# First attention chunk, w_in block shape, planner constants and priorities changed in a fused attention, MoE and SoLU kernel

## The chip, the core and the metric

The kernel is one program on one core of a Trainium2 chip. Five engines work beside each other, each through its own list of instructions in the order in which they were emitted: TensorE (PE, with its weight loads as PEld), VectorE (DVE), ScalarE (ACT), GpSimd (POOL) and SyncE (SP), which here issues all DMAs. The metric is the device time of one execution in microseconds (us), the median of several runs.

## What is computed

Three layers follow one another. Everything is float32 at the program's edge; the products are made of a rounded high part and a low part of each operand.

```python
# q, k, v: (2, 8, 768, 64); proj: (64, 6)
q_bits = (einsum('bhsd,dk->bhsk', q, proj) > 0);  k_bits = same of k
q_bucket = sum(q_bits * 2**arange(6));  k_bucket = same
scores = where(q_bucket[..., :, None] == k_bucket[..., None, :], q @ k.T / 8, -1e9)
x = softmax(scores) @ v                      # to (1536, 512): 8 heads of 64
p = domain_probs / sum(domain_probs)         # 4 experts
y = sum_e p[:, e] * (relu(x @ w1[e]) @ w2[e])  # w1: 4 x 512 x 1024
h = y @ w_in                                 # 512 x 1024
z = h * softmax(h);  ln = (z - mean) / sqrt(var + 1e-6) * g_ln
out = ln @ w_out                             # 1024 x 512
```

## The kernel before

The 1536 tokens are four chunks of 384 (three tiles of 128 each); chunks 0 and 1 are batch 0, chunks 2 and 3 batch 1. Of each chunk the kernel does attention over eight heads, the four experts (`moe_a` is x @ w1, `moe_b` is h @ w2), then y @ w_in (`h2_piece`, `h2_mm`), the normalisation (`ln_tiles`) and the product with w_out (`ln_a`, `ln_b`). Attention of chunk 0 (`attn_first`) has nothing to run beside. Attention of chunk c + 1 (`attn_steps`, handed out by `fill`) is interleaved with the experts of chunk c. The last chunk ends in `last_layer`, which goes tile by tile.

**Chunk 0.** `proj_steps` takes one head at a time: POOL rounds k or q to its high part, DVE subtracts to get the low part (tile `hl`), PE transposes both, ACT copies them into a "stack" of high over low (`k_stk`, `q_stk`, which live in the buffers wsa, wsb, stk and kC), and PE multiplies the stack with `lhs_w` to get the hash bits, added up over a group of heads in one PSUM tile. When a group is whole, ACT and DVE turn it into rows of 0 and -C (k) or 1 and 0 (q) for 16 contraction rows per head (`k_br`, `q_br`: the tiles ee and vs, and qC). The group size is `GS`: heads 0 to GS - 1 are projected before the first head's scores, the others are steps of a generator (`rest`) that the first heads' rows call. `unit(h)` loads head h's second operands by DMA: kB from the stack's low part and the bits, qB likewise. Each row tile `rr` of a head then makes four matmuls of scores (two halves, stack and kB/qB), DVE takes the maximum (tile `sm`), ACT the exponential (tile `p`), POOL divides, PE transposes p, ACT and DVE write high and low part, and a head ends in 12 matmuls with v (tile `vs`). At `h == GS` the kernel stores all eight k stacks and their bits to the DRAM tile kD, for chunk 1.

**w_in.** It arrives as 64-bit numbers; `decode_a` writes it to the DRAM tile winD in four blocks. `Stream` loads a block into `wra`, ACT rounds it to the high part and DVE subtracts (`wsa`). `h2_mm(c, t, j, o)` uses block j for tile t: 12 matmuls of 256 columns.

**Order.** Nothing is issued while the functions run: `Recorder.add` notes every operation, and `emit` then plays a list schedule with assumed costs and hand-over times (`cost`, `HOPS`, and in `emit` the time for a DMA to land and an extra for results that TensorE waits for) and issues each engine's instructions in the order of that play. Which ready operation goes first is its place in the recording, less `ahead(...)`, plus `SHIFTS`: rows of (engine, first, end, places) that move all operations first to end. On the chip the order is then fixed; only semaphores delay an instruction.

All operations carry the line of `emit`'s last loop, L406, so the rows below tell them apart by tile: `xh,wsa` is `moe_a`, `wsb,hh` is `moe_b`, `wsa,xh` is `h2_mm`, `idr,hl` and `lhs_w` are the projections, `idn,p` the transposes of p, `idn,y` those of y, `idn,ln` those of the normalised tile.

Of the kernel before, what the change touches and what calls it, by code (L numbers as in the profile page):

```python
# [95 lines left out]
class Recorder:  # L96
# [198 lines left out]
    def emit(self):  # L295
# [46 lines left out]
        while len(order) < n:  # L342
# [9 lines left out]
            for e in ready:  # L352
# [26 lines left out]
                if e == "S":  # L379
                    free[e] = now + (1.2 if o["turn"] else 0.46)  # L380
                    wire = max(wire, now + 1.15) + (0.75 if o["turn"] else o["cost"])
                    done = wire + 0.85
# [9 lines left out]
                for j in users[i]:  # L392
# [3 lines left out]
                    if e != "T" and "T" in ops[j]["forms"]:  # L396
                        hop += 0.4
# [12 lines left out]
def lsh_attention_moe_solu(  # L410
# [34 lines left out]
    GS = 4  # L445
# [77 lines left out]
    def f(ap):  # L523
        return ap.bitcast(F32)
# [255 lines left out]
    def attn_first():  # L780

        c = 0
# [17 lines left out]
        load_k(2, GS)  # L800
# [73 lines left out]
        for h in range(H):  # L874
            nxt = unit(h + 1) if h + 1 < H else None
            if h == GS:
                rec.gate = marks[-1]
                for g in range(H):
                    SP.dma_start(out=kD[b][0:2 * D, g], in_=f(k_stk[g]))
                    SP.dma_start(out=kD[b][2 * D:LQ, g], in_=k_br[0 if g < GS else 1][g:128:H])  # L880
                rec.gate = None
# [80 lines left out]
    winD = dram.tile([FF2 // 256, 128, KD, 256], F32, name="winD")  # L962
# [45 lines left out]
    def decode_a():  # L1008
# [3 lines left out]
        for j in range(FF2 // n):  # L1012
            for kk in range(KD):
                dst = winD[j * n // 256:(j + 1) * n // 256, :, kk].rearrange("j p n -> p j n")
# [7 lines left out]
    class Stream:  # L1022
# [10 lines left out]

        def load(self, i):
            while self.nl <= min(i, len(self.items) - 1):
                t = wr_r[self.kind].next()
# [4 lines left out]
        def split(self, i):  # L1041
            while self.ns <= min(i, len(self.items) - 1):
                self.load(self.ns)
                w = self.place.get(self.ns) or ws_r[self.kind].next()
                t = self.raw.pop(self.ns)
# [139 lines left out]
    def h2_mm(c, t, j, o):  # L1185
        yh, yl = xT[c]
        wh, wl = W1.get(i1["in", c, j])
        ts = slice(t * 128, t * 128 + 128)
        m = 0
# [293 lines left out]
```

## Time and profile before

| | |
|---|---|
| median of 3 runs | 947.25 us (946.66 to 950.53) |
| profiled execution | 946.51 us, of it a span of 944.7 us from first to last instruction |
| PE busy | 900.8 us (95%), 4864 matmuls |
| DVE, ACT, POOL busy | 673.1, 612.0, 144.1 us |
| mean granted TensorE clock | 0.991 of full speed |

A row of a timeline tells when a run of equal instructions started, how long it lasted, and in brackets how long the engine sat idle before it and what ended that. Consecutive matmuls overlap, so their durations don't add up: what one costs is the distance between starts.

### The profile page before, as it was taken

Reading aid. Unit: us, or ns where it says so; the run is one execution under the profiler, and the core shown is the slowest. Engines: PE = TensorE matmul, PEld = TensorE weight load, DVE = VectorE, ACT = ScalarE, POOL = GpSimd, SP = SyncE. Lnnn points to the kernel's source line nnn. Section 1 sums busy time; section 2 is a strip of 40 time slices with the busy share of each in tenths; the row PEclk is TensorE's granted clock in tenths of the full one; section 3 lists DMA queues with packets and bytes.
Section 4 is the critical chain, followed back from the end, with each engine's and each line's share of the span. In section 5 each row is a group of like instructions: output and inputs, shape, how many; then the busy total and the mean of one; then the engine's idle time right before and its main releaser. Section 6 shows DMA issues by size and latency. Waiting matters only on the chain.

```text
span 944.7 us, 14178 instructions
## 1 busy us (share of the span) xinstructions
PE 900.8 (95%) x4864; PEld 807.4 (85%) x4864; DVE 673.1 (71%) x1178; ACT 612.0 (65%) x1072; POOL 144.1 (15%) x180
## 2 busy tenths in 40 slices
PE   6788999999998999999999999999999999999998
PEld 5676798889897988888898998899898998999886
DVE  5775776999998897778784789568674564454564
ACT  4786647889874667777874599667773464333442
POOL 4453211102222210311212011111110000000000
PEclk9989999999999999999999999999999999999999
DMA  7156889999996978999998599689863343533500
GB/s 199 37 191 178 267 273 198 263 282 253 286 309 211 288 246 216 227 233 214 224 251 228 158 213 231 184 211 210 174 162 112 113 133 112 166 116 109 179 23 34
DMA packets 216808, 182.19 MB, mean 193 GB/s; under 512 B 127520, under 2 KB 183712, under 8 KB 216736
## 3 DMA queue, kind: packets, MB, share of 16 engines
q1 hardware_dynamic: 216736, 181.29, 71.7%
q8 instruction: 38, 0.62, 0.3%
q14 instruction: 34, 0.28, 0.1%
HBM read 127.89 MB, written 22.09 MB: 159 GB/s over the span
## 4 chain that ended last, share of the span: by engine, by line
PE 66%; ACT 13%; DVE 9%; DMA 6%; issue 4%; SPq 1%; POOL 1%; ACTq 0%; DVEq 0%; POOLq 0%
PE PS L406 66%; ACT p L406 4%; DMA t<-l 2%; DVE sm L406 2%; ACT h L406 1%; ACT t L406 1%; DMA t<-h 1%; ACT ee L406 1%; ACT wsb L406 1%; ACT sm L406 1%; ACT wsa L406 1%; DVE l L406 1%; DVE ln L406 1%; DVE wsa L406 1%; DMA vr<-in_q_dram 1%
## 5 line engine op out<-in xcount | busy, mean ns | idle before, releaser
L406 PE MATMUL PS<-wsb,hh 128*128 128x512 f32 x928 | 291.5, 395 | 2.6 <-ACT y L406 1.6
L406 PE MATMUL PS<-xh,wsa 128*128 128x384 f32 x1024 | 284.0, 338 | 0.6 <-DVE hx L406 0.6
L406 PEld LDWEIGHTS PS<-wsb,hh 128*128 128x128 f32 x928 | 169.9, 188 | 29.4 <-ACT y L406 2.6
L406 PEld LDWEIGHTS PS<-xh,wsa 128*128 128x128 f32 x1024 | 188.0, 188 | 6.2 <-DVE hx L406 1.4
L406 PE MATMUL PS<-wsb,hx 128*128 128x512 f32 x464 | 182.6, 394 | 0.0
L406 PE MATMUL PS<-xl,wsa 128*128 128x384 f32 x512 | 172.4, 337 | 0.0
L406 ACT ACTIVATE hh<-PS 128x384 fp32r<-128x384 f32 (+2 forms) x162 | 77.4, 483 | 107.0 <-PE PS L406 104.5
L406 DVE SCALAR_TENSOR_TENSOR hx<-PS,hh 128x384 fp32r<-128x384 f32 x128 | 70.3, 552 | 92.6 <-ACT hh L406 92.3
L406 DVE TENSOR_TENSOR wsb<-wrb,wsb 128x1024 fp32r<-128x1024 f32 x78 | 96.3, 1236 | 24.2 <-ACT wsb L406 24.2
L406 DVE TENSOR_TENSOR wsa<-wra,wsa 128x1024 fp32r<-128x1024 f32 x78 | 95.7, 1226 | 21.7 <-ACT wsa L406 21.6
L406 DVE TENSOR_REDUCE sm<-PS 128x1 f32<-128x768 f32 x96 | 90.9, 950 | 20.7 <-PE PS L406 20.3
L406 ACT ACTIVATE wsb<-wrb 128x1024 fp32r<-128x1024 f32 x78 | 82.4, 1056 | 33.6 <-PE PS L406 28.2
L406 PEld LDWEIGHTS PS<-wsb,hx 128*128 128x128 f32 x464 | 87.0, 188 | 18.9
L406 PEld LDWEIGHTS PS<-xl,wsa 128*128 128x128 f32 x512 | 96.4, 188 | 4.0
L406 ACT ACTIVATE p<-PS,sm 128x768 f32<-128x768 f32 x96 | 94.9, 989 | 2.4 <-DVE qC L406 0.5
L406 ACT ACTIVATE wsa<-wra 128x1024 fp32r<-128x1024 f32 x78 | 82.2, 1054 | 18.8 <-PE PS L406 13.0
L406 DVE SCALAR_TENSOR_TENSOR l<-p,sm,h 128x768 f16<-128x768 f32 x72 | 78.2, 1087 | 14.8 <-ACT h L406 13.8
L406 POOL TENSOR_SCALAR t<-t 128x2304 fp32r<-128x2304 f16 x23 | 52.2, 2271 | 227.7 <-DMA t<-h 97.6
L406 ACT ACTIVATE h<-p,sm 128x768 f16<-128x768 f32 x72 | 67.1, 932 | 16.4 <-DVE sm L406 16.4
L406 ACT ACTIVATE sm<-sm 128x1 f32<-128x1 f32 x192 | 45.9, 244 | 35.5 <-DVE sm L406 31.3
L406 PE MATMUL PS<-kB,qB 80*128 80x384 f32 x192 | 65.9, 343 | 0.0
L406 PE MATMUL PS<-t,vs 128*128 128x384 f32 x312 | 59.3, 338 | 4.5 <-ACT stk L406 2.9
(169 smaller groups left out, 1260.0 us busy)
## 6 DMA issues: line engine op xcount, KB each, us to landing
wra<-in_moe_w_dram SPq DMA_DIRECT2D x64, 512.0 KB, 4.3
wrb<-in_moe_w_dram SPq DMA_DIRECT2D x64, 512.0 KB, 4.3
kC<-kD SPq DMA_DIRECT2D x24, 384.0 KB, 4.5
wra<-winD SPq DMA_DIRECT2D x16, 512.0 KB, 4.0
wrb<-woutD SPq DMA_DIRECT2D x16, 512.0 KB, 4.2
kB<-kD SPq DMA_DIRECT2D x24, 240.0 KB, 4.6
vr<-in_v_dram SPq DMA_DIRECT2D x28, 192.0 KB, 4.0
qD<-stk SPq DMA_DIRECT2D x27, 192.0 KB, 4.5
```

Source lines behind the costliest of these rows:

```text
L406: fn(**{key: x.at(x.slot.base) if isinstance(x, View) else x for key, x in kw.items()})
```

## The change

Five things are edited; a sixth follows from them.

1. `GS` goes from 4 to 2: the hash bits of heads 0 and 1 are a group of their own, heads 2 to 7 are the second. The loads of q and k follow: k of heads 0 and 1 singly, q of 0 and 1, then k of 2 to 7 and q of 2 to 7 in one DMA each. All of `rest` is called within head 0.
2. The k stacks go to kD two heads at a time at heads 3, 4, 5 and 6, each pair gated on the row before.
3. winD's blocks are 256 rows by 512 columns. `h2_mm` makes six matmuls of 512 columns for (tile, j), two j add up in one bank; `as_item` reshapes the same buffers.
4. The planner's constants: issuing a DMA 0.46 to 0.5 us (a transposing one 1.2 to 1.3), its landing 1.0 us later, the extra for TensorE 0.4 to 0.2 us.
5. `SHIFTS` has 43 other rows in place of 33.

```diff
 SHIFTS = (
-    ("T", 1885, 2035, -40), ("T", 3698, 3758, 40), ("T", 642, 792, -5), ("T", 1328, 1728, -40),
...
+    ("T", 3046, 3446, 20), ("T", 2487, 2893, 20), ("A", 3613, 3910, -20), ("T", 2298, 2698, -40),
...
@@ emit
                 if e == "S":
-                    free[e] = now + (1.2 if o["turn"] else 0.46)
+                    free[e] = now + (1.3 if o["turn"] else 0.5)
                     wire = max(wire, now + 1.15) + (0.75 if o["turn"] else o["cost"])
-                    done = wire + 0.85
+                    done = wire + 1.85
...
                     if e != "T" and "T" in ops[j]["forms"]:
-                        hop += 0.4
+                        hop += .2
...
-    GS = 4
+    GS = 2
...
         load_k(1, 2)
-        load_k(2, GS)
         load_q(0, GS)
         load_k(GS, H)
         load_q(GS, H)
...
-            if h == GS:
+            for g in range(*{3: (0, 2), 4: (2, 4), 5: (4, 6), 6: (6, 8)}.get(h, (0, 0))):
                 rec.gate = marks[-1]
-                for g in range(H):
-                    SP.dma_start(out=kD[b][0:2 * D, g], in_=f(k_stk[g]))
-                    SP.dma_start(out=kD[b][2 * D:LQ, g], in_=k_br[0 if g < GS else 1][g:128:H])
+                SP.dma_start(out=kD[b][0:2 * D, g], in_=f(k_stk[g]))
+                SP.dma_start(out=kD[b][2 * D:LQ, g], in_=k_br[0 if g < GS else 1][g:128:H])
                 rec.gate = None
...
-    winD = dram.tile([FF2 // 256, 128, KD, 256], F32, name="winD")
+    winD = dram.tile([FF2 // 256, 128, 2, 512], F32, name="winD")
...
-                dst = winD[j * n // 256:(j + 1) * n // 256, :, kk].rearrange("j p n -> p j n")
+                dst = winD[j * (KD // 2) + kk // 2][:, kk % 2]
...
+        def as_item(self, x, i):
+
+            a = self.items[i].shape[1]
+            return x if x.shape[1] == a else x.rearrange("p k n -> p (k n)").rearrange("p (a n) -> p a n", a=a)
...
-        m = 0
+        m = j % 2 * 6
         with rec.group():
-            for kk in range(KD):
+            for kk in range(2):
                 for a, w in ((yh, wh), (yh, wl), (yl, wh)):
-                    T.matmul(out=o, lhsT=a[:, kk, ts], rhs=w[:, kk, :], start=(m == 0), stop=(m == 3 * KD - 1))
+                    T.matmul(
+                        out=o, lhsT=a[:, j % 2 * 2 + kk, ts], rhs=w[:, kk, :], start=(m == 0), stop=(m == 3 * KD - 1)
+                    )
                     m += 1
...
-            h2_mm(c, t, j, o[:, j % 2 * 256:j % 2 * 256 + 256])
+            h2_mm(c, t, j, o)
...
-                h2_mm(c, t, j, h[:, j // 2, j % 2 * 256:j % 2 * 256 + 256])
+                h2_mm(c, t, j, h[:, j // 2])
```

What moves, at three places. **At the start, on SP** (ln holds k, y holds q, vr and wrb hold v of single heads, wsa0 is the stack of head 0). Before:

```order
L406 DMA ln0_113<-in_k_dram 128x384
L406 DMA ln0_113<-in_k_dram 128x2x384
L406 DMA y0_112<-in_q_dram 128x4x192
L406 DMA ln0_113<-in_k_dram 128x4x384
L406 DMA y0_112<-in_q_dram 128x4x192
L406 DMA vr0_72<-in_v_dram 128x384
L406 DMA vr1_73<-in_v_dram 128x384
L406 DMA wrb0_104<-in_v_dram 128x6x64 x2
L406 DMA wrb1_105<-in_v_dram 128x6x64
L406 DMA kB0_125<-wsa0_106 64x768
```

and now:

```order
L408 DMA ln0_113<-in_k_dram 128x384
L408 DMA vr0_72<-in_v_dram 128x384
L408 DMA y0_112<-in_q_dram 128x2x192
L408 DMA ln0_113<-in_k_dram 128x6x384
L408 DMA y0_112<-in_q_dram 128x6x192
L408 DMA vr1_73<-in_v_dram 128x384
L408 DMA wrb0_104<-in_v_dram 128x6x64 x2
L408 DMA wrb1_105<-in_v_dram 128x6x64 x2
L408 DMA kB0_125<-wsa0_106 64x768
```

The q of the first group is half as large and stands ahead of the large k; the load of kB still stands behind all of k, q and v. On PE, the last rows before the first scores (the pair wsa0 with wsb0, then kB0 with qB0, is a score) were

```order
L406 MATMUL PS_63<-wsb0_108,lhs_w_124 128x384 x4
L406 MATMUL PS_63<-idr_121,hl0_64 128x128 x6
L406 MATMUL PS_63<-idr_121,hl1_65 128x128 x6
L406 MATMUL PS_63<-wsb1_109,lhs_w_124 128x384 x4
L406 MATMUL PS_63<-idr_121,hl0_64 128x128 x6
L406 MATMUL PS_63<-stk0_66,lhs_w_124 128x384 x2
L406 MATMUL PS_63<-idr_121,hl1_65 128x128 x6
L406 MATMUL PS_63<-idr_121,hl0_64 128x128 x3
L406 MATMUL PS_63<-wsa0_106,wsb0_108 128x384
L406 MATMUL PS_63<-kB0_125,qB0_127 128x384
```

and are now

```order
L408 MATMUL PS_63<-wsa0_106,lhs_w_124 128x384 x2
L408 MATMUL PS_63<-wsb0_108,lhs_w_124 128x384 x2
L408 MATMUL PS_63<-idr_121,hl0_64 128x128 x6
L408 MATMUL PS_63<-idr_121,hl1_65 128x128 x6
L408 MATMUL PS_63<-wsa1_107,lhs_w_124 128x384 x4
L408 MATMUL PS_63<-idr_121,hl0_64 128x128 x6
L408 MATMUL PS_63<-idr_121,hl1_65 128x128 x6
L408 MATMUL PS_63<-wsb1_109,lhs_w_124 128x384 x4
L408 MATMUL PS_63<-idr_121,hl0_64 128x128 x6
L408 MATMUL PS_63<-idr_121,hl1_65 128x128 x6
L408 MATMUL PS_63<-wsa0_106,wsb0_108 128x384
L408 MATMUL PS_63<-kB0_125,qB0_127 128x384
```

All eight heads of k (six transposes each) still come first, but of q only heads 0 and 1, where it was five heads; the bits of the first group are whole after the second row here.

**At the end of chunk 0's experts, on PE** (t320 with vs1 is a head's product with v; xh1 with wsa0 is `moe_a` of chunk 1). Before:

```order
L406 MATMUL PS_63<-idr_121,hl1_65 128x128 x3
L406 MATMUL PS_63<-t320_86,vs1_75 128x384 x12
L406 MATMUL PS_63<-stk0_66,lhs_w_124 128x384 x2
L406 MATMUL PS_63<-idr_121,hl0_64 128x128 x6
L406 MATMUL PS_63<-xh1_96,wsa0_106 128x384
```

and now:

```order
L408 MATMUL PS_63<-idr_121,hl0_64 128x128 x3
L408 MATMUL PS_63<-stk0_66,lhs_w_124 128x384 x2
L408 MATMUL PS_63<-t320_86,vs1_75 128x384 x12
L408 MATMUL PS_63<-stk1_67,lhs_w_124 128x384 x2
L408 MATMUL PS_63<-idr_121,hl1_65 128x128 x6
L408 MATMUL PS_63<-xh1_96,wsa0_106 128x384
```

Two matmuls more stand between a projection's transposes and the product with v; six transposes in a row remain.

**In the last layer, on PE** (t320 with xh1 is `h2_mm` of tile 0). Before:

```order
L406 MATMUL PS_63<-idn_120,y0_112 128x128 x4
L406 MATMUL PS_63<-wsb1_109,hh_110 128x512 x2
L406 MATMUL PS_63<-wsb1_109,hx_111 128x512
L406 MATMUL PS_63<-wsb1_109,hh_110 128x512 x2
L406 MATMUL PS_63<-wsb1_109,hx_111 128x512
L406 MATMUL PS_63<-idn_120,y0_112 128x128 x4
L406 MATMUL PS_63<-t320_86,xh1_96 128x256 x2
```

and now:

```order
L408 MATMUL PS_63<-idn_120,y0_112 128x128 x4
L408 MATMUL PS_63<-wsb0_108,hh_110 128x512 x2
L408 MATMUL PS_63<-wsb0_108,hx_111 128x512
L408 MATMUL PS_63<-wsb1_109,hh_110 128x512 x2
L408 MATMUL PS_63<-wsb1_109,hx_111 128x512
L408 MATMUL PS_63<-wsb1_109,hh_110 128x512 x2
L408 MATMUL PS_63<-wsb1_109,hx_111 128x512
L408 MATMUL PS_63<-t320_86,xh1_96 128x512 x2
L408 MATMUL PS_63<-t320_86,xl1_98 128x512
L408 MATMUL PS_63<-t320_86,xh1_96 128x512 x2
L408 MATMUL PS_63<-t320_86,xl1_98 128x512
L408 MATMUL PS_63<-idn_120,y0_112 128x128 x4
```

Nine matmuls instead of six follow the first tile's transposes, and tile 1's transposes stand behind six of tile 0's; tile 2's have moved likewise from behind all of tile 1 into its first quarter. On DVE, at the same place, before (wsb0 is a split of w_out, xl1 the low part of the transposed y):

```order
L406 SCALAR_TENSOR_TENSOR y0_112<-PS_63,pr_131,y0_112 128x512 x2
L406 TENSOR_TENSOR wsb0_108<-wrb1_105,wsb0_108 128x1024
L406 TENSOR_TENSOR xl1_98<-PS_63,xh1_96 128x4x128
L406 SCALAR_TENSOR_TENSOR y0_112<-PS_63,pr_131,y0_112 128x512
L406 TENSOR_TENSOR wsb1_109<-wrb0_104,wsb1_109 128x1024
```

and now:

```order
L408 SCALAR_TENSOR_TENSOR y0_112<-PS_63,pr_131,y0_112 128x512 x2
L408 TENSOR_TENSOR xl1_98<-PS_63,xh1_96 128x4x128
L408 TENSOR_TENSOR wsb0_108<-wrb1_105,wsb0_108 128x1024
L408 SCALAR_TENSOR_TENSOR y0_112<-PS_63,pr_131,y0_112 128x512
L408 TENSOR_TENSOR wsb1_109<-wrb0_104,wsb1_109 128x1024
```

The low part of y now goes ahead of the split; the same two have changed places on ACT. And the product with w_out of tile 0 now follows its transposes (idn with ln0, eight) at once, where 12 matmuls of `h2_mm` stood between.

## Rows read from the trace of the kernel before

**Rows 1.** The page, part 1: busy time, share, instructions.

```profile
PE 900.8 (95%) x4864; PEld 807.4 (85%) x4864; DVE 673.1 (71%) x1178; ACT 612.0 (65%) x1072; POOL 144.1 (15%) x180
```

**Rows 2.** Windows: stretch, length, busy time (count) by engine, clock, DMA share, GB/s.

```profile
24.18:108.79 84.61, 72.39 (x372) 56.86 (x372) 56.75 (x113) 62.55 (x157) 35.13 (x62) 0.95 0.51 158
108.79:301.00 192.21, 185.12 (x966) 167.59 (x965) 165.73 (x277) 143.36 (x244) 36.39 (x36) 0.99 0.98 259
```

**Rows 3.** Waits of PE from 108.79 us on: total us, times, longest.

```profile
PE PS L406 <- ACT p L406: 5.3, 8, 1.5
...
PE PS L406 <- DMA kC<-kD: 0.3, 1, 0.3
```

**Rows 4.** Lines by form, PE, the matmuls of 256 columns: count, busy us, mean ns.

```profile
L406 PE MATMUL PS<-wsa,xh 128*128 128x256 f32 x336 | 61.7, 285 | 0.0
...
L406 PE MATMUL PS<-t,xl 128*128 128x256 f32 x24 | 6.9, 287 | 0.3 <-DVE xl L406 0.3
```

**Rows 5.** Timeline of PE, late in the experts and in the last layer.

```profile
896.18 0.62 PE L406 MATMUL PS<-wsb,hh 128*128 128x512 f32 x2
...
898.91 0.60 PE L406 MATMUL PS<-idn,y 128*128 128x128 f32 x4
...
902.50 0.48 PE L406 MATMUL PS<-t,xh 128*128 128x256 f32 x2
...
914.09 0.60 PE L406 MATMUL PS<-idn,y 128*128 128x128 f32 x4
```

**Rows 6.** Timeline of SP at the start: issue time, length of the run of issues.

```profile
3.54 0.47 SPq L406 DMA_DIRECT2D y<-in_q_dram  x1
...
6.55 6.17 SPq L406 DMA_DIRECT2D wrb<-in_v_dram  x3
...
20.12 1.17 SPq L406 DMA_DIRECT2D qB<-qC  x2
```

**Rows 7.** Timeline of all engines, 14 to 25 us.

```profile
16.59 1.96 DVE L406 TENSOR_SCALAR ee<-p 64x768 fp32r<-64x768 f32 x2
...
18.58 1.13 DVE L406 TENSOR_SCALAR qC<-p 64x384 fp32r<-64x384 f32 x2
...
21.02 1.00 PE L406 MATMUL PS<-idr,hl 128*128 128x128 f32 x6 [2.79 <-DVE hl L406]
...
24.18 0.65 PE L406 MATMUL PS<-wsa,wsb 128*128 128x384 f32 x1
```

**Rows 8.** Timelines of SP and PE around the k stores.

```profile
69.94 0.54 SPq L406 DMA_DIRECT2D kB<-stk  x1
...
78.39 0.42 PE L406 MATMUL PS<-stk,kC 128*128 128x384 f32 x1
```

**Rows 9.** Timeline of PE: waits in the middle of the program.

```profile
286.86 2.38 PE L406 MATMUL PS<-t,vs 128*128 128x384 f32 x12 [1.32 <-ACT stk L406]
...
355.29 0.73 PE L406 MATMUL PS<-wsb,hh 128*128 128x512 f32 x2 [1.42 <-ACT y L406]
...
523.94 0.44 PE L406 MATMUL PS<-stk,lhs_w 128*128 128x384 f32 x1 [0.68 <-ACT stk L406]
```

**Rows 10.** Timelines of PE and DVE in the last layer.

```profile
902.08 0.66 PE L406 MATMUL PS<-idn,y 128*128 128x128 f32 x4 [1.18 <-DVE xl L406]
...
915.38 0.50 PE L406 MATMUL PS<-t,xh 128*128 128x256 f32 x2 [0.69 <-ACT xh L406]
...
900.20 1.22 DVE L406 TENSOR_TENSOR wsb<-wrb,wsb 128x1024 fp32r<-128x1024 f32 x1 [1.02 <-ACT wsb L406]
901.34 0.68 DVE L406 TENSOR_TENSOR xl<-PS,xh 128x512 fp32r<-128x512 f32 x1
...
921.84 1.28 DVE L406 TENSOR_TENSOR hx<-PS,hh 128x512 fp32r<-128x512 f32 x2
```

**Rows 11.** DMA issues: KB each, median us from issue to landing.

```profile
wra<-in_moe_w_dram SPq DMA_DIRECT2D x64, 512.0 KB, 4.3
...
t<-h SPq DMA_TRANSPOSE x72, 4.4
```

More of the change, by code (lines that the diff above doesn't have):

```diff
@@ L1032, in __init__ @@
             self.ns = 0
+        def as_item(self, x, i):
+            a = self.items[i].shape[1]
+            return x if x.shape[1] == a else x.rearrange("p k n -> p (k n)").rearrange("p (a n) -> p a n", a=a)
         def load(self, i):
             while self.nl <= min(i, len(self.items) - 1):
-                t = wr_r[self.kind].next()
+                t = self.as_item(wr_r[self.kind].next(), self.nl)
                 SP.dma_start(out=t, in_=self.items[self.nl])
@@ L1044, in split @@
                 w = self.place.get(self.ns) or ws_r[self.kind].next()
+                w = [self.as_item(x, self.ns) for x in w]
                 t = self.raw.pop(self.ns)
@@ L1388, in lsh_attention_moe_solu @@
     for j in range(2):
-        W1.place[i1["in", NC - 1, j]] = halves(t32[:, j, 0:1024], t32[:, j, 1024:2048], KD)
+        W1.place[i1["in", NC - 1, j]] = halves(t32[:, j, 0:1024], t32[:, j, 1024:2048], 2)
     dead = NC % 2
```

18 rows, old and new, of the table SHIFTS are left out of this document.

## The prediction, made before the changed kernel was run

> **What bounds the kernel now.** Part 1 of the page comes first: PE is busy for 900.8 of 944.7 us [rows 1]. The windows by stage tell two kinds of stretch apart. From 24.18 to 108.79 us, attention of chunk 0 with nothing beside it, PE is busy for 72.39 of 84.61 us, ACT for 62.55 and DVE for 56.75: no engine is full, a chain from engine to engine sets the pace. From 108.79 to 301.00 us PE is busy for 185.12 of 192.21 [rows 2]; there PE's own work is the time, and a gain is PE work that is gone or a wait of PE that is filled. The list of PE's waits after 108.79 us has nine rows, the first 5.3 us (the exponential not ready) and the last 0.3; they add up to 18.6 us [rows 3]. So a new order without less work can give at most 18.6 us behind chunk 0's attention.
>
> **The change part by part.** All sums go against the profiled execution, 946.51 us (its span of 944.7 and 1.8 around it). The median of the runs, 947.25, lies 0.7 above; I add that at the end.
>
> *w_in in blocks of 512 columns.* The lines by form hold four rows of 256-column matmuls, 336 + 168 + 48 + 24 = 576 [rows 4]; now there are 288 of 512 columns. Price of the old: from 902.50 to 914.09 us PE runs 96 of them without a wait, 11.59 / 96 = 0.1207 us each. Price of the new, from the experts' 512-column matmuls: 12 from 896.18 to 898.91 us, 2.73 / 12 = 0.2275 [rows 5]. A pair of old ones costs 0.2414, so each new one saves 0.0139, and 288 save 4.0 us. The stretch is short, though, and a new block waits for weights from the same splits; three quarters of these matmuls stand where PE is full [rows 2]. I take 3.2, and as ends 2.0 and 4.0.
>
> Here the Trainium skill speaks otherwise. In "TensorE: Matmul & The Clock Gate", section "Back-to-back issue gap", it gives about 131 ns per matmul of 512 columns for a sustained stream of weight loads and matmuls, and N/2.4 + 2.5 ns for one alone. By the first, 288 matmuls would take 37.7 us and the gain would be some 31 us, an estimate from that page; by the second the saving is 2.5 ns for each matmul that is gone, 0.7 us. This trace has 0.2275 us in a sustained stream and so bears out neither.
>
> *winD's stores and loads* move the same bytes in as many DMAs. Their cover is the stretch in which they run, hundreds of us ahead of their use, and I cost them at nothing; in the worst case it is one load's landing, 4.3 us [rows 11].
>
> *The last layer.* PE waits 1.18 us at 902.08, for the low part xl of the first transposed tile, because DVE does a split of w_out (1.22 us long, from 900.20) ahead of it. At 915.38 it waits 0.69 for ACT's high part of tile 2's transposes, which stand directly ahead of their use [rows 10]. In the new order xl goes ahead of the split, nine matmuls (2.1 us at 0.2275) cover it, and tile 2's transposes stand 18 matmuls, 4.1 us, ahead of their use. Both waits, 1.87 us, should go. What is late next: the product with w_out of tile 0 now follows its transposes at once. ACT's copy and DVE's subtraction (1.28 us for two in a row at 921.84, so 0.64 for one [rows 10]) are then uncovered; the second group of transposes covers about half. I charge 0.5. Net -1.4, ends -1.9 and +0.6.
>
> *Hash bits of two heads first.* In the old order DVE turns the first group's sums into bits from 16.59 to 19.71 us; the next k head's low part waits behind it, and PE sits idle for 2.79 us until 21.02; the first score starts at 24.18 [rows 7]. With two heads in the group the sums are whole after four transposed heads instead of eight, so DVE does the bits while PE and POOL wait for the large loads, and they no longer delay the other k heads. But the loads of kB and qB, bits last, are queued on SP behind all first loads. These hold SP until 12.72 us (three issues lasted 6.17 from 6.55), and the pair of issues for the bits of q starts at 20.12 [rows 6]. Counted in the order, the same number of issues stands ahead, and v's fourth load more. So the operands come at most some 1 us earlier, and what PE saves is mainly the q transposes that no longer stand ahead: the first score may start 1 to 3 us earlier. I take 2.0. Ends: 3.9 (the whole wait of 2.79 and 1.1 of the queue) and a loss of 4.0: the second group's bits, of six heads now, are wanted at head 2 instead of head 4, and their q part is made among the rows of heads 0 and 1, where ACT is 74% busy [rows 2]. If they come late, kB and qB of head 2 wait on SP, with the operands of head 3 behind them, and all rows with them.
>
> Three q heads' projections move from ahead of the first score to behind it, and the bits of the second k group move the other way; I count these as even.
>
> *k stacks over four heads.* In the old order 16 stores stand in a row on SP, and the load of kB for head 6 follows them at 69.94 us. Its first score runs at 78.39 [rows 8], over 8 us later. Spread out, each kB load has at most four stores ahead instead of 16, but the load was not what head 6 waited for: 0 us. Ends: 0 and, if a store of the last pair delays head 7's operands by two issues of 0.54, +1.1.
>
> *Planner constants and the priority table.* They take away no work. The landing of a DMA is assumed 1.0 later: a 512 KB weight load at 1.15 + 1.85 + 0.85 = 3.85 us before and 4.85 now, a transpose 2.75 and 3.75; measured are 4.3 and 4.4 [rows 11]. So for transposes the plan is nearer to the trace, for weights it errs to the safe side. What the new order fills, read at three waits of PE [rows 9]: at 286.86 (1.32, a product with v behind a projection's copy) two matmuls more lie between and 0.3 goes; the waits right behind it, up to 299.40, lose about 0.7, since 12 matmuls of `moe_a` now lie between two projections; at 355.29 (1.42) six more transposes and four matmuls of scores go first, but two of the transposes wait for a PSUM bank, so 0.4 goes; at 523.94 (0.68) six matmuls lie between and 0.5 goes. That is 1.9. The other waits have about the same rows ahead as before. A new order also opens waits that I can't see; I charge 0.3. Net -1.6, ends: -9 (half of the 18.6) and +14.4 (the third rival below).
>
> **Sum:** -3.2 - 1.4 - 2.0 - 0 - 1.6 = -8.2; 946.5 - 8.2 = 938.3 for the profiled kind of execution, and 0.7 more, **939.0 us**, for the median.
>
> **The rivals.**
>
> *A. Only PE work counts; the head start is lost.* The first score is bound by SP's queue [rows 6] and the chain through chunk 0 gives the rest back; the new table fills some waits and opens as many. For it: no engine is full there [rows 2], so an earlier start may only lengthen waits further on. Against it: DVE's 2.79 us [rows 7] do stand on the path. Left are w_in and the last layer, 3.2 + 1.4: 947.25 - 4.6 = 942.6, on the edge of what can be told.
>
> *B. The table fills half of PE's waits.* 43 rows can move more than the three places that I read, and landing times near the measured ones [rows 11] help everywhere. Against it: the scores of one tile and the next have about 4.1 us of PE work between them in either order. Time: 947.25 - 3.2 - 1.4 - 2.0 - 9 = 931.6.
>
> *C. Slower: the extra for TensorE is now too small.* The plan lets PE take a result 0.2 us sooner than before. There are 72 row tiles in chunks 1 to 3, each with a score that waits for the exponential ahead of it; if every one is put 0.2 us too early, PE waits 72 x 0.2 = 14.4 us more: 947.25 - 3.2 - 1.4 - 2.0 + 14.4 = 955.0. It decides against the change once over 0.16 us of the 0.2 per tile is really waited (11.4 in all, enough to eat the 6.6 and reach 952). Against it: the exponential was the reason for only 5.3 us of waits in the old order [rows 3], so most scores have slack.
>
> *D. Head 2's bits come late.* The start costs 4.0 instead of giving 2.0: 939.0 + 6.0 = 945.0.
>
> **How the numbers follow.** What a measurement of this kernel can tell from no change is about 0.5%, 4.7 us: below 942.5 is faster, above 952.0 slower. Forecast 0.52, all of it faster (935 to 942). A 0.20, half on either side of 942.5. B 0.10, faster. C 0.12, slower. D 0.06, within. Faster: 0.52 + 0.10 + 0.10 = 0.72. Same: 0.10 + 0.06 = 0.16. Slower 0.12. The range leaves out C and half of B, 0.17: 931 to 946, which holds D, and A with w_in at its low end.
>
> **What would show it.** In the changed kernel's trace: 288 `h2_mm` matmuls at 0.226 to 0.234 us between starts (w_in); the first score between 21 and 23 us, and the first matmul of `moe_a` at 105 to 108 instead of 108.79 (start; A if it is back at 108.5, D if a score of head 2 waits for a DMA); no wait for xl ahead of tile 0 of the last layer, and one of 0.3 to 0.8 ahead of the first product with w_out; PE's waits after the first `moe_a` at 14 to 18 us in place of 18.6 (B if under 10, C if over 25, most of it for the exponential). The prediction is wrong above all if chunk 0's attention ends by more than 4 us elsewhere than I say: that chain runs through every engine, and I have read its order at its start alone.

## The result, and the profile after

The changed kernel takes 936.32 us (median; 935.08 to 940.70) against 947.46 for the one before: a ratio of 0.9885, 95% interval 0.9845 to 0.9925. Run once more (first experiment) it took 938.49, ratio 0.9878 (0.9831 to 0.9924). So it is faster by 1.2%, 11 us; 939.0 was forecast, and the range was 931 to 946.

Both executions of the changed kernel that were profiled can be set beside the one of before. "Again" is the first experiment; `yT` is the first transpose of y in a layer.

| stretch | before | changed | again | forecast |
|---|---|---|---|---|
| start to first score | 24.18 | 23.70 | 23.04 | 21 to 23 |
| start to first `moe_a` | 108.79 | 102.53 | 102.38 | 105 to 108 |
| first `moe_a` to `yT` of layer 0 | 189.60 | 190.53 | 189.39 | |
| to `yT` of the last layer | 600.52 | 601.45 | 599.73 | |
| last layer | 45.79 | 44.39 | 44.40 | |
| span | 944.7 | 938.9 | 935.9 | |

The page of the changed kernel, part 1 (it answers to [rows 1]): PE has 288 matmuls fewer and 9.3 us less of busy time.

```profile
PE 891.5 (95%) x4576; PEld 789.2 (84%) x4576; DVE 682.0 (73%) x1178; ACT 611.7 (65%) x1072; POOL 149.3 (16%) x180
```

Waits of PE in the changed kernel from its first `moe_a` on (total us, times, longest), to be read beside [rows 3]. They add up to 22.1 us (20.8 in the second execution) where 18.6 stood before and 14 to 18 was forecast; the exponential p has grown most.

```profile
PE PS L408 <- ACT p L408: 8.5, 10, 2.0
PE PS L408 <- DVE hx L408: 2.6, 3, 1.1
PE PS L408 <- DMA qB<-qD: 2.2, 1, 2.2
...
PE PS L408 <- DVE st L408: 1.4, 1, 1.4
PE PS L408 <- DVE y L408: 1.2, 2, 0.8
PE PS L408 <- DVE wsa L408: 1.0, 1, 1.0
```

Timeline of PE in the changed kernel (start, us, ..., wait). The first two rows answer to [rows 7]: the wait for hl (the low part of a k head) at the start is longer now, 5.25 us, and the first score comes only 0.48 earlier. From 731.37 to 747.80 run 72 of the new 512-column matmuls without a wait. The last three answer to [rows 10].

```profile
16.79 0.97 PE L408 MATMUL PS<-idr,hl 128*128 128x128 f32 x6 [5.25 <-DVE hl L408]
...
23.70 0.41 PE L408 MATMUL PS<-wsa,wsb 128*128 128x384 f32 x1
...
731.37 0.71 PE L408 MATMUL PS<-wsa,xh 128*128 128x512 f32 x2
...
747.80 0.33 PE L408 MATMUL PS<-xh,wsa 128*128 128x384 f32 x1
...
894.51 0.60 PE L408 MATMUL PS<-idn,y 128*128 128x128 f32 x4
...
904.32 0.60 PE L408 MATMUL PS<-idn,y 128*128 128x128 f32 x4
...
916.81 0.50 PE L408 MATMUL PS<-xh,hh 128*128 128x512 f32 x1 [1.44 <-DVE st L408]
```

SP's queue at the start of the changed kernel (it answers to [rows 6]): four loads of v hold SP now, and the pair of issues for the bits of q stands at 20.50 instead of 20.12.

```profile
5.71 8.86 SPq L408 DMA_DIRECT2D wrb<-in_v_dram  x4
...
20.50 1.17 SPq L408 DMA_DIRECT2D qB<-qC  x2
```

DVE and POOL at the same time, ahead of the wait of 5.25 us: DVE makes the bits of the first group (p, ee, qC) from 11.78 to 15.37. The low part of the next k heads, whose high part POOL begins at 12.43, stands behind them and starts at 15.39.

```profile
11.78 1.41 DVE L408 TENSOR_TENSOR p<-PS,p 64x768 f32<-64x768 f32 x2 [2.38 <-ACT p L408]
12.43 0.99 POOL L408 TENSOR_SCALAR hl<-ln 128x384 fp32r<-128x384 f32 x2 [3.25 <-DMA ln<-in_k_dram]
...
14.43 0.94 DVE L408 TENSOR_SCALAR qC<-p 64x384 fp32r<-64x384 f32 x2
...
15.39 1.72 DVE L408 TENSOR_TENSOR hl<-ln,hl 128x384 fp32r<-128x384 f32 x2
```

DVE and ACT ahead of the wait at 916.81 in the last layer: on DVE a split of w_out and a maximum stand in front of the subtractions that the product with w_out needs; the subtractions also need ACT's copies (hh).

```profile
914.28 1.22 DVE L408 TENSOR_TENSOR t<-wrb,t 128x1024 fp32r<-128x1024 f32 x1
...
915.48 0.68 DVE L408 TENSOR_REDUCE mx<-PS 128x1 f32<-128x512 f32 x1
916.07 0.68 DVE L408 TENSOR_TENSOR hx<-PS,hh 128x512 fp32r<-128x512 f32 x1
...
915.02 1.08 ACT L408 ACTIVATE hh<-PS 128x512 fp32r<-128x512 f32 x2
```

**Where the 6.3 us up to the first `moe_a` come from.** Windows (stretch, length, busy time and count of PE, PEld, DVE, ACT, POOL, granted clock, DMA share, GB/s) of the whole start, before and then changed:

```profile
0.00:108.79 108.79, 87.50 (x451) 69.96 (x452) 69.89 (x140) 73.42 (x179) 46.69 (x87) 0.94 0.56 166
```

```profile
0.00:102.53 102.53, 80.91 (x451) 65.73 (x452) 68.81 (x138) 71.91 (x178) 45.60 (x87) 0.98 0.60 179
```

PE runs 451 matmuls in both. It is idle for 108.79 - 87.50 = 21.3 us before and 102.53 - 80.91 = 21.6 after: no less waiting in sum. The same matmuls only take 6.6 us less, at a mean clock of 0.98 instead of 0.94. Before, the clock is at its lower level, 0.50 (1.2 GHz), in stretches such as these; PE had waited 1.19 us up to 45.61 and 0.90 up to 47.48, and 1.10 up to 65.89 and 0.33 up to 67.18:

```profile
46.00:48.00 2.00, 1.10 (x7) 0.79 (x6) 1.58 (x5) 1.33 (x4) 1.48 (x4) 0.71 0.00 1
48.00:50.00 2.00, 2.00 (x13) 2.00 (x11) 1.11 (x3) 1.97 (x6) 1.13 (x2) 0.50 0.30 80
68.00:70.00 2.00, 2.00 (x10) 1.90 (x9) 1.20 (x2) 1.77 (x4) 1.25 (x3) 0.50 0.88 326
```

In the second execution of the changed kernel the clock is full between 25 and 75 us:

```profile
25.00:50.00 25.00, 19.07 (x118) 15.70 (x117) 20.56 (x42) 21.05 (x56) 11.95 (x24) 1.00 0.20 50
50.00:75.00 25.00, 22.48 (x139) 20.17 (x138) 19.14 (x41) 23.13 (x63) 15.89 (x27) 1.00 0.60 190
75.00:100.00 25.00, 23.44 (x114) 17.14 (x113) 14.70 (x28) 17.29 (x39) 8.58 (x14) 0.93 0.87 282
```

Why it falls there and not here is not settled, and the order alone does not decide it. Some kernels of the experiments below have, up to some point, the same order of instructions on all five engines, and so show what one order does in several executions:

| order at the start, execution | first score | first `moe_a` | PE busy up to it | clock |
|---|---|---|---|---|
| before | 24.18 | 108.79 | 87.50 | 0.94 |
| the same order: w_in's blocks alone | 22.25 | 107.50 | 86.06 | 0.94 |
| changed | 23.70 | 102.53 | 80.91 | 0.98 |
| the same order: again | 23.04 | 102.38 | 81.27 | 0.98 |
| the same order up to 97 us: five rows of the table | 24.30 | 103.09 | 80.80 | 0.98 |
| the same order as five rows: six rows of the table | 24.27 | 106.42 | 85.40 | 0.94 |

PE's idle time up to the first `moe_a` is 21.0 to 22.3 us in all six, so what differs is mostly PE's busy time, that is, the clock. In the execution with six rows PE waits 1.05 us up to 40.62 and 0.62 up to 42.39, as the changed kernel does (1.05 up to 40.05, 0.62 up to 41.82). There the clock falls, while the three others of this order keep it. The same five microseconds with six rows and in the second execution of the changed kernel:

```profile
43.00:48.00 5.00, 4.77 (x20) 4.17 (x19) 3.27 (x7) 4.08 (x10) 3.38 (x6) 0.50 0.34 84
```

```profile
43.00:48.00 5.00, 3.98 (x26) 3.31 (x26) 4.08 (x9) 4.93 (x14) 3.65 (x7) 1.00 0.25 67
```

So one order differs between executions at the first `moe_a` by 1.3 us (old) and by up to 4.0 (new), and at the first score by up to 1.9. All four executions of the new order are ahead of both of the old one at the first `moe_a`, by 1.1 to 6.4 us. How much of the 6.3 is the order's and how much the execution's stays open. The mean clock over the whole span, which is on record for every execution, is 0.988 to 0.995 in eight of the changed kernel (0.991 in the mean) and 0.987 to 0.996 in 44 of the kernel before (0.990). A start at 0.98 instead of 0.94 would by itself raise it by 0.04 x 102.5 / 937 = 0.004, an estimate; so a usual execution need not have the start that was profiled.

### The profile page after: what moved, and what is told of

Read it like the earlier page. It is cut to its first block, busy times and chain, and to the rows that moved or that the text cites. A ratio compares the mean times of both kernels' runs of the same rounds, so it can differ in the third digit from the quotient of the medians.

```text
span 938.9 us, 13595 instructions
## 1 busy us (share of the span) xinstructions
PE 891.5 (95%) x4576; PEld 789.2 (84%) x4576; DVE 682.0 (73%) x1178; ACT 611.7 (65%) x1072; POOL 149.3 (16%) x180
## 4 chain that ended last, share of the span: by engine, by line
PE 72%; DVE 12%; ACT 7%; issue 4%; DMA 2%; SPq 1%; POOL 1%; DVEq 0%; ACTq 0%; POOLq 0%
PE PS L408 72%; ACT p L408 2%; DVE l L408 2%; DVE sm L408 2%; DVE ln L408 1%; DVE y L408 1%; SPq L408 1%; DVE hx L408 1%; DVE wsb L408 1%; DMA t<-l 1%; DVE wsa L408 1%; ACT sm L408 1%; DVE st L408 1%; ACT ee L408 1%; ACT h L408 1%
## 5 line engine op out<-in xcount | busy, mean ns | idle before, releaser
L408 DVE TENSOR_TENSOR wsa<-wra,wsa 128x1024 fp32r<-128x1024 f32 x78 | 97.8, 1255 | 28.3 <-ACT wsa L408 28.0
L408 DVE SCALAR_TENSOR_TENSOR l<-p,sm,h 128x768 f16<-128x768 f32 x72 | 83.2, 1156 | 10.3 <-ACT h L408 10.1
```

Source lines behind the costliest of these rows:

```text
L408: fn(**{key: x.at(x.slot.base) if isinstance(x, View) else x for key, x in kw.items()})
```

## The experiments

The theory to be tested first: the two groups of heads make the gain at the start, w_in's blocks and the last layer the rest. Its rival: the parts of the change are worth little by themselves, and the table's rows, fitted to this kernel, make the gain.

**The changed kernel again.** No edit.

> The changed kernel once more, unedited, to see which of its waits are its own. Its profiled execution (span 938.9 us) was the longest of four, the others had 933.3 to 935.4. Theory 1 (the order opened new waits behind chunk 0's attention): PE's waits after the first moe_a add up to about 22 us again, in the same places (203.79, 249.65, 354.71, 398.04). Theory 2 (part of them belonged to that execution): a span of 933 to 936, and waits of 17 to 19 us, without the 2.2 us for qB's DMA at 354.71. In both the first moe_a runs at 102.5.

938.49 us; the profiled span is 935.9. PE's waits are 20.8 us, in the same places: 1.41 us at 204.03, 2.00 at 249.90, 2.05 at 352.96 (qB's DMA), 1.48 at 396.92. The waits are the kernel's own, as Theory 1 has it, though the span is the one that Theory 2 expected.

**Empty tables.** The changed kernel, and later the one before, with

```
-SHIFTS = ( ... )
+SHIFTS = ()
```

> The changed kernel with an empty priority table; everything else as changed. Theory 1 (the two groups, the spread stores and the planner's constants make the 6.3 us of chunk 0's attention): the first moe_a still runs at 102 to 104 us, and the loss is in the later waits of PE: 945 to 960 in all. Theory 2 (the table's rows make it, by entries below place 1000): the first moe_a falls back to 106 to 109.

> The kernel before with an empty priority table. The changed kernel with an empty table took 972.4 us, 36 more than with it. Theory 1 (each table is fitted to its own kernel, and the parts of the change that are no table are worth little alone): this one also takes 965 to 980, with its first moe_a at 109 to 114 us. Theory 2 (the new table is the better one, the old one did less): this one takes 950 to 960, so that the other parts of the change together cost time.

The changed kernel: 972.38 us, ratio 1.0236 (1.0178 to 1.0293); first `moe_a` at 107.98. The one before: 954.25 us, 1.0068 (1.0039 to 1.0097). Theory 2 is met in both: in the changed kernel the table is worth 36 us, in the one before 6, and all other parts of the change together cost 18 us as long as no table is fitted to them. At the start the theory of the groups finds no support: without the table nearly nothing of the 6.3 us is left in the profiled execution (107.98 against 108.79; the one before has 106.53 without its table), though the first score comes earlier there (21.40 us) than with it (23.70). Again it is the clock: 451 matmuls, 22.3 us idle, but 85.68 busy.

```profile
0.00:107.98 107.98, 85.68 (x451) 69.54 (x452) 67.14 (x138) 71.58 (x178) 48.07 (x87) 0.91 0.56 170
```

**k stacks at once; four heads in the group.** Both against the changed kernel with the empty table.

```
-            for g in range(*{3: (0, 2), 4: (2, 4), 5: (4, 6), 6: (6, 8)}.get(h, (0, 0))):
+            if h == 4:
                 rec.gate = marks[-1]
-                SP.dma_start(...)
+                for g in range(H):
+                    SP.dma_start(...)
```

> The changed kernel with an empty table, and the k stacks stored all at once at head 4 as in the kernel before. Against the changed kernel with an empty table: by the prediction (the stores cost nothing) the first score of head 6 and the first moe_a stand within 1 us of that kernel's; if the stores held up head 6, both come 3 to 7 us later.

```
-    GS = 2
+    GS = 4
...
         load_k(1, 2)
+        load_k(2, GS)
```

> The changed kernel with an empty table and four heads in the first group, with the k load of heads 2 and 3 back. Against the changed kernel with an empty table: by the prediction (two heads first give 2 us at the first score) the first score is 1 to 3 us later and the first moe_a 2 us later. Rival: the first score moves by under 0.6 us, as in the changed kernel (23.70 against 24.18), and what the group gives or costs shows among heads 1 to 5.

Stores at once: 972.51 us, the same as with them spread (972.38), but the first `moe_a` stands at 104.60 instead of 107.98. Most of that is not the stores' doing: the first place where any engine's order differs is on SP, and SP's last issue ahead of it already stands at 47.73 instead of 50.47. So 2.7 of the 3.4 us belong to the execution, and for the stores some 0.6 is left, within the 1.1 that I had as their bound. Four heads: 974.43 us, 1.0253 (1.0205 to 1.0301); first score at 22.14 instead of 21.40, first `moe_a` at 108.79 instead of 107.98. These 0.8 us at either place are less than one order differs between executions, so the 2.0 of the group of two is not seen here, nor any other worth of it.

**Five rows of the table.** Only the rows for places below 526, where chunk 0's attention ends:

```
+SHIFTS = (
+    ("S", 47, 67, -20), ("T", 508, 513, 40), ("S", 5, 25, 20), ("T", 406, 426, 2), ("T", 496, 646, 20),
+)
```

> The changed kernel with only those five rows of its table that begin below place 526, where chunk 0's attention ends. If these five make the gain in chunk 0's attention (with no table its first moe_a stood at 108.0, with all rows at 102.4), the first moe_a is at 102 to 103.5, and the whole is 5 us below the 972.4 of the empty table: 965 to 969. If rows for later work make it, by holding chunk 1's projections back, it stays at 105 to 108.

967.87 us; first `moe_a` at 103.09, and the clock up to there is 0.98:

```profile
0.00:103.09 103.09, 80.80 (x452) 65.70 (x452) 68.36 (x138) 71.88 (x178) 47.21 (x87) 0.98 0.59 177
```

As expected, then, but the kernel with a sixth row, which has the same order up to here, stands at 106.42. That the five rows bring the gain at the start is likely, three executions of four having it, and not shown; the whole is 4.5 us below the 972.38 of the empty table, with ranges that overlap (963.59 to 971.24 and 970.13 to 975.47). The other 38 are worth 967.87 - 937.4 (mean of the two medians of the changed kernel) = 30 us behind it.

**w_in's blocks alone, in the kernel before.** Its diff is the eight places of the change that name `winD`, `as_item`, `h2_mm` and `halves(..., 2)`; for instance

```
-    winD = dram.tile([FF2 // 256, 128, KD, 256], F32, name="winD")
+    winD = dram.tile([FF2 // 256, 128, 2, 512], F32, name="winD")
```

> The kernel before with w_in in blocks of 512 columns and nothing else. By the prediction 3.2 us less (2.0 to 4.0), in matmuls of w_in alone: the stretch from the first yT of the last layer to the end is 0.6 us shorter, and chunk 0's attention is unchanged to 0.3 us. Rival: the planner's order changes with the new costs and gives or takes more than that: under 940 or over 948.

947.32 us, ratio 0.9989 (0.9966 to 1.0012): no difference that can be measured; 3.2 us less would be 0.9966, at the edge of the interval. The matmuls get cheaper as in the changed kernel: 227 ns between the starts of two (median), 120 for the old ones. Up to `yT` of layer 0 PE's order is that of the kernel before; behind it, w_in's matmuls left out, 211 of 2890 places hold another matmul. The stretch from there to the last layer is 603.46 us long against 600.52, though three layers' share of w_in, 2.9 us, should have made it shorter; the last layer is 0.33 us shorter, not 0.6. So a new order that takes back what the block size gives is likely, as the rival has it, though its times (under 940 or over 948) are not met. But the profiled execution (951.33) is near the top of its ten, 944.31 to 951.84, and is 3.5 us longer in the stretch ahead of `yT` too, with the same order there; so how much of it is the order stays open.

**Constants of the planner.** In the changed kernel with its table, with the empty one, and only the extra for TensorE with the empty one:

```
-                    free[e] = now + (1.3 if o["turn"] else 0.5)
+                    free[e] = now + (1.2 if o["turn"] else 0.46)
...
-                    done = wire + 1.85
+                    done = wire + 0.85
...
-                            hop += .2
+                            hop += 0.4
```

> The changed kernel, its table too, with the planner's old constants (issue 0.46, landing 0.85, extra 0.4 for TensorE). Theory 1 (the constants are worth under 2 us by themselves, as the prediction's charge for them): 934 to 940. Theory 2 (table and constants are fitted together): another order everywhere, 940 to 955, with PE's waits after the first moe_a at over 25 us instead of 21 to 22. Theory 3 (the smaller extra for TensorE makes the 7.3 to 8.5 us of waits for the exponential, 5.3 before): these fall under 5 and the time to 931 to 935.

> The changed kernel with an empty table and the planner's old constants. With empty tables the changed kernel took 972.4 us and the one before 954.3, so the parts that are no table cost 18 us. Theory 1 (the new constants cost it): this one takes 950 to 957, and from 275 to 300 us PE's busy time is back at 20 us or more (15.54 in the changed kernel with an empty table, 20.34 in the one before with an empty table). Theory 2 (w_in's blocks, the two groups or the spread stores cost it): 966 to 975.

> The changed kernel with an empty table and only the extra for TensorE back at 0.4; the DMA constants stay new. The prediction's third rival (an extra of 0.2 is too small, 14.4 us) gives 955 to 960, with PE's waits after the first moe_a far below those of the changed kernel with an empty table. If the later landing of DMAs in the plan is what costs, it stays at 968 to 975.

With its table: 964.96 us, 1.0168 (1.0111 to 1.0226), above all three theories; PE's waits behind the first `moe_a` are 33.2 us, as the second has it. With the empty one: 973.35 us, where the new constants have 972.38; only the extra for TensorE: 974.86. Set against the kernel before, run beside them, these are 1.0289 (1.0261 to 1.0316), 1.0236 (1.0178 to 1.0293) and 1.0311 (1.0285 to 1.0338), intervals that overlap. So by themselves the constants are worth nothing that can be told, and my rival C, 14.4 us for too small an extra, is refuted where no table hides it. But 43 rows that fit one set of constants are worth 8 us instead of 36 with the other (11 and 34 by the ratios).

**Two halves joined.** New rows and constants up to place 526, old rows and constants behind it:

```
+    ("S", 47, 67, -20), ("T", 508, 513, 40), ("S", 5, 25, 20), ("T", 406, 426, 2), ("T", 496, 646, 20),
+    ... (the old rows, one place lower)
...
-                    done = wire + 1.85
+                    done = wire + (1.85 if i < 526 else 0.85)
... (likewise the issue time and the extra for TensorE)
```

> The changed kernel, planned in two parts: up to place 526, where chunk 0's attention ends, with the new constants and the five rows of the new table that begin there; behind that with the old constants and the rows of the old table, one place lower, since the changed kernel has one instruction less ahead of them. If the new table's rows for later work and the new constants cost time behind chunk 0 (PE's waits there 21 to 22 us in the changed kernel, 18.6 before), this one is faster than the changed kernel: the first moe_a at 102 to 104, waits of 18 to 20, 931 to 935 us. If the old rows fit the old instruction costs only, the order comes out another way and it takes 940 to 950.

970.36 us, 1.0252 (1.0237 to 1.0268): far above both expectations, with the first `moe_a` at 105.14 and PE's waits behind it at 34.9 us, although chunks 1 to 3 have the old rows and the old constants, and w_in's blocks alone did not hurt these. On a plan that starts otherwise the old rows are worth nothing: without any for chunks 1 to 3 (and with the new constants) it was 967.87.

**What the 30 us behind the start are.** In the kernels that lost, one seam stands out: from the first score of chunk 1's last head to `yT` of layer 0, where chunk 2's q projections begin. The experts of layer 0 have 696 matmuls to fill PE beside that attention. Counted along PE's matmuls, 570 are gone by that score in the kernel before and 564 in the changed one, but 630 with five rows or no table and 645 in the joined kernel. The count is not all: the kernel before with an empty table has 585 and lost only 6 us, the changed one with the old constants has 591 and lost 28. Windows of the two stretches, cut at the second matmul of that score: the kernel before,

```profile
108.79:255.38 146.59, 143.24 (x741) 129.72 (x741) 125.28 (x214) 111.97 (x191) 24.80 (x26) 1.00 1.01 260
255.38:298.39 43.01, 39.65 (x208) 36.13 (x208) 38.54 (x59) 28.77 (x50) 11.08 (x9) 0.96 0.90 265
```

and the changed one with five rows:

```profile
103.09:259.69 156.60, 153.85 (x798) 140.69 (x798) 140.24 (x225) 114.66 (x198) 31.85 (x28) 1.00 0.97 252
259.69:306.81 47.12, 35.79 (x148) 31.63 (x148) 29.93 (x52) 26.82 (x43) 7.19 (x8) 0.75 0.71 207
```

With five rows PE does 57 matmuls more ahead of the score and has 60 fewer behind it; there it idles for 47.12 - 35.79 = 11.3 us instead of 3.4, and the clock falls to 0.75, so that 148 matmuls take nearly as long as 208. To test the count, one more row of the table was added, which brings one step of the experts' second product forward and lowers the count from 630 to 582:

```
-    ("T", 496, 646, 20),
+    ("T", 496, 646, 20), ("T", 1020, 1025, -40),
```

> The changed kernel with six rows of its table: the five for chunk 0's attention, and the one that brings one step of the experts' second product, place 1024, 40 places forward. In TensorE's order of layer 0 the experts have 696 matmuls; ahead of the first score of chunk 1's last head stand 570 of them in the kernel before, 564 in the changed one, 630 with the five rows alone, and 582 with this sixth row. Theory 1 (the stretch from that score to the first yT has too little experts' work left, and PE waits and loses its clock): PE's waits in that stretch fall from the 11.3 us of the five rows to 3 to 6, the stretch from the first moe_a to the first yT from 203.7 us to 189 to 195, and the whole from 967.9 to 953 to 959. Theory 2 (the count is a symptom, and the attention there is late for another reason, DVE or the DMAs): waits of 9 us or more, and 963 to 970.

965.16 us, 1.0172 (1.0144 to 1.0200): between the theories in waits, and in time with the second. The profiled executions of this kernel and of the one with five rows (971.49 and 971.24) are the longest of their seven and four, so their windows may show more loss than a usual execution has. Windows and a wait of this kernel:

```profile
106.42:261.27 154.85, 148.33 (x765) 135.76 (x765) 134.90 (x222) 113.23 (x197) 34.92 (x29) 0.98 0.97 253
261.27:307.36 46.09, 38.94 (x184) 34.43 (x184) 35.13 (x54) 25.65 (x43) 9.32 (x8) 0.85 0.76 218
```

```profile
212.39 0.80 PE L399 MATMUL PS<-wsb,hh 128*128 128x512 f32 x1 [3.06 <-DVE wsb L399]
```

The seam's idle time falls to 7.2 us and its clock rises to 0.85, so the count has a part in what PE waits for there; that it is worth anything in the whole is not shown (965.16 against 967.87, with ranges that overlap). And the step that was brought forward now stands ahead of its weights' split on DVE, PE waits 3.06 us, and the attention is as late as before (154.85 against 156.60). The changed kernel reaches the score in 147.4 us, with further rows of its table for VectorE, SyncE and TensorE. What the rest of the 30 us is, kernel by kernel, stays open, and so does which part of the change upsets the plan without a table: undoing the stores, the group or the constants one at a time changed nothing (972 to 975), and w_in's blocks with an empty table, or two parts undone at once, were not run.

None of these kernels beats the changed one.

## Why the prediction held, by its own steps

The time was right, and so was the mechanism of two terms; two other terms were wrong, in opposite directions, by 4.4 and 3.4 us, and that they nearly cancel is luck. Against the profiled 944.7, with the second execution of the changed kernel (935.9, -8.8) for measured:

| term | forecast | measured |
|---|---|---|
| w_in | -3.2 | -3.8 |
| last layer | -1.4 | -0.4 |
| start (with the k stores) | -2.0 | -6.4 |
| planner and table | -1.6 | +1.8 |
| sum | -8.2 | -8.8 |

The planner's row is what is left of the span when the others are taken off. The start's row is that of one execution; by the four of this order it lies between -1.1 and -6.4.

*w_in*: the mechanism held. 16.43 us for 72 matmuls is 0.2282 each, inside the 0.226 to 0.234 that were to show it, against 0.2414 for a pair of old ones ([rows 5]); 288 x 0.0132 = 3.8. This is the price of the matmuls; alone in the kernel before the blocks gave no gain that could be measured (0.9989). The 131 ns that the Trainium skill gives ("TensorE: Matmul & The Clock Gate", section "Back-to-back issue gap") are not reached in the changed kernel either.

*Last layer*: it is 1.39 us shorter, but 72 x 0.0132 = 0.95 of that is w_in's. Both waits of [rows 10] are gone, 1.87 us, as was read from the order; what comes late next was found at the right place, the first product with w_out, but it waits 1.44 us and not 0.5. I had costed one copy and one subtraction, taken half of them as covered by the second group of transposes, and not looked at what stands ahead of the subtraction on DVE: a split of w_out of 1.22 us, the very thing that had made the old wait for xl, and behind it a maximum. ACT's first copy is done by about 915.6 (half of its two from 915.02 to 916.10); the subtraction starts only when the maximum is over, at 916.07, and with its 0.68 us leads to PE's start at 916.81.

*Start*: the step that failed is "the first score may start 1 to 3 us earlier", and that this would be the gain. It started 0.5 to 1.1 earlier, and even that is less than one order differs there (24.18 and 22.25 before). What went wrong is the sentence that DVE makes the bits while PE and POOL wait for the large loads and no longer delays the other k heads: DVE is at them until 15.37, 3 us after POOL had the next k to round (12.43), so the low part comes late again and PE waits 5.25 us instead of 2.79. At the first score itself PE waits for nothing: it works from 16.79 to 23.70 without an idle time above 0.2 us. SP's issues for the bits of q came no sooner either, as [rows 6] let one expect. PE's idle time up to the first `moe_a` did not fall at all. The 6.4 of the table is the granted clock, which my sum had no term for: I priced waits and matmuls, and let the clock stay as it was. [rows 2] already showed it (0.95 in chunk 0's attention, 0.99 behind it), and I read there only that no engine is full. With the new order the start had the higher clock in three executions of four. The k stores, which I costed at 0, show no cost beyond 0.6 us.

*Planner and table*: the step that failed is reading a few waits to be filled as the gain, with 0.3 us for all that a new order opens. Of the three waits, 286.86 has shrunk to 0.60 and 523.94 to 0.35 (second execution), as forecast; but at the third, where 1.42 was to shrink, PE now waits three times, 0.96, 1.12 and 2.05 us (the last for qB at 352.96). The waits behind 286.86, of which 0.7 was to go, stay (1.82 and 1.91 us). So the very places that I read, forecast at -1.9, gave +1.8; ahead of the last layer PE's waits add up to 19.3 us where 16.5 stood, and p costs 7.3 us instead of 5.3. Measured against the kernel before, the new order costs 1.8 us behind chunk 0 (4.7 in the first execution). Of what the table does, this is the small remainder: the other parts cost 18 us until it is fitted, and it is worth 36.

*The signs*: the spacing of w_in's matmuls and the missing wait for xl came true. The first score (23.0 to 23.7), the first `moe_a` (102.4 to 102.5), the wait ahead of the first product with w_out (1.44) and PE's waits (20.8 to 22.1) lie outside what was to show. And the sign named above all, chunk 0's attention ending more than 4 us elsewhere than said, was met: 106.8 by the sum, 102.4 to 102.5 in the two executions.

The rivals: A holds that only PE's work counts and the head start is lost, and what it says of waits is true, ahead of the first `moe_a` and behind it; the clock is what it leaves out. B fell (waits of 21 to 22 us, not 9), and C's price fell with the run that has the extra at 0.4 (974.86, not faster than 972.38). D shows, but small: the first score of head 2 waits 0.62 us at 41.82 for the bits of q, not the 4.0 that I had as its price.

## What to carry to other kernels

An order that was tuned by a table belongs to one kernel: after any change of structure, costs or constants, compare with empty tables on both sides, or the parts can't be told from the fit. Where TensorE's stretch is bound by a chain, add a term for its clock: count matmuls and idle time on both sides, and where these agree the rest is the clock. Then look at more than one execution of the same order, before a few microseconds in one stretch are put down to an edit. Filler work beside a chain has to last until the chain ends; a count of what is left at the chain's last link is a quick look, but moving a filler forward also moves it ahead of its operands.

## What the hardware showed that was not expected

A wait of PE can cost more than its length. With five rows, the stretch from the first `moe_a` to `yT` takes 203.7 us against 189.6: PE idles 14.1 us instead of 6.7, but it is also busy for 189.6 instead of 182.9 with 945 matmuls instead of 948. Nearly half of the loss is the clock. The kernel with the empty table shows the level directly, between and behind waits of 0.6 to 2.2 us:

```profile
284.00:287.00 3.00, 1.77 (x7) 1.58 (x8) 2.75 (x5) 1.34 (x4) 0.69 (x1) 0.50 0.31 118
287.00:290.00 3.00, 3.00 (x11) 3.00 (x10) 1.53 (x3) 0.38 (x1) 0.62 (x1) 0.50 0.91 205
```

In 3.00 us of uninterrupted work PE does 11 matmuls there: 12 of this kind (t with vs) take 4.21 us from 285.85, and 2.38 at a clock of 1.00 in the kernel before ([rows 9], at 286.86). The Trainium skill ("TensorE: Matmul & The Clock Gate", section "HAM oscillation — how this bites in real kernels") tells of a loop that waits some 3 to 5 us for its DMA at every turn and loses the clock each time. These rows show the lower level among shorter waits, in a kernel whose PE is 94% busy. And one order, behind the same waits up to 42 us, kept the clock in three executions and lost it in a fourth, as the table of the start has it.
